# The first loads in smaller pieces: x's first columns ahead of wq, and wq's last chunks behind a DMA transpose

## The chip, the cores and the metric

The kernel runs on one core of one Trainium2 chip. The metric is the time of one execution on the device in microseconds (us); lower is better. The core has a matrix engine (TensorE, PE in the profile, with PEld for its weight loads), VectorE (DVE), ScalarE (ACT), GpSimd (POOL), and SyncE (SP), which here only issues DMAs. PE works on operands in on-chip memory and writes to eight banks of accumulation memory ("ps"), each of 128 x 512 fp32; DVE and ACT read the banks out. DMAs are issued by SP and ACT, each into a queue of its own, and both queues are served by the same 16 DMA engines.

## The reference

x is 2048 x 512. Two branches work on the same x and are mixed by a gate per row:

```python
g = _sigmoid((x * gate_w).sum(-1, keepdims=True))
a = _A_ref(x, A_wq, A_wk, A_wv, A_wo, A_beta)
b = _B_ref(x, B_W_gate, B_W_up, B_W_down)
return g * a + (1 - g) * b
```

`_A_ref` is attention with 32 heads of 16 columns, in four segments of 512 rows. In each segment there is a causal softmax over the segment itself, and a linear "memory" of all segments before: q and k pass through phi(t) = t + 1 where t > 0, else exp(t); M and z sum phi(k)^T v and phi(k); the memory's answer is phi(q) M / (phi(q) z). The two answers are mixed by a gate per head (from beta), and multiplied by wo. `_B_ref` is a feed-forward layer: relu(x W_gate) * (x W_up), times W_down, with 1792 inner columns. All weights and x are bf16.

## The kernel before

The work is a list of tasks: each task has an engine, a duration as its author reckons with it, the tasks it depends on, and a function that emits its instructions. The order in which the tasks are emitted is written out (`ORDER`, lines 30 to 93), and so is the choice of buffers (`UNITS`, lines 95 to 103). Each engine runs its instructions in that order, and semaphores make it wait for what it needs. So nothing is reordered at run time: an instruction that waits holds up all that stand behind it on its engine.

For q, k and the feed-forward layer x is needed transposed, as `xT`, with the 512 columns of x as four chunks of 128 partitions. q is projected in four column blocks c of 128 (8 heads each). Each block adds up four matmuls of 128 x 512, one for each chunk ci: weights `wq_sb[:, ci, block]`, moving operand `xT[:, ci, :]`. A projection can be emitted in full form (line 469) or as four matmuls of 32 columns (line 473), which run side by side; the second form is taken where the work before it ran in that mode. Score matmuls (lines 626 and 639), the sums over values (line 699) and the memory's matmuls (lines 755, 795, 819) work on parts of the matrix engine. Scores are kept in banks 0 to 3, where ACT takes the exponential of 2048 columns at once (line 648); the other work goes through banks 4 to 7 from then on.

The start of the first segment is made by hand, and it is there that the change lies:

- Warm-up (`heat`, lines 910 to 916): PE multiplies constants, six matmuls of 512 columns and one of 128, while the first loads are on their way.
- x's first 256 columns come as plain loads into `xn`, rows as partitions: "n0" (row tiles 0 and 1) in SP's queue, "n1" (row tiles 2 and 3) in ACT's (lines 300 and 301). PE transposes them by matmuls with an identity (`flip`, lines 504 to 508); DVE copies the tiles of n0 out into `xT[0]`, and ACT those of n1 (line 521).
- x's last 256 columns come through a DMA transpose straight into `xT[0]` (line 304), in SP's queue.
- wq's chunk 0 is loaded in SP's queue ahead of that transpose and chunk 1 in ACT's (lines 302 and 303); chunks 2 and 3 follow as one load in ACT's queue (line 306). wk in two halves, wv and all else follow in SP's queue.
- PE projects q with chunk 0 for all four blocks, then with chunk 1, then, for each block, with chunks 2 and 3 (lines 549 to 554). DVE copies each block out (line 559). k follows: DVE copies it out (line 575) and makes three masked forms of it (line 578), which the first score matmuls need.

```python
    got_n[0] = [load_x0(eng, 2 * t, 2 * t + 2, halves[0], "n%d" % t)
                for t, eng in enumerate((nc.sync, nc.scalar))]
    got_q = [load(eng, wq_sb[:, ci, :], A_wq[ci * P:(ci + 1) * P, :], "q%d" % ci)
             for ci, eng in enumerate((nc.sync, nc.scalar))]
    nc.sync.dma_start_transpose(out=xT[0][:, NC // 2:NC, :], in_=x[0:L, halves[1]])
    got_x0b = arrival("x0")
    got_q.append(load_rows(nc.scalar, wq_sb, A_wq, 1, "q"))
```

`LANDS` (line 258) are the arrival times of the loads that the written order was made with; they set nothing at run time.

Of the kernel before, what the change touches and what calls it, by code (L numbers as in the profile page):

```python
# [12 lines left out]
P = 128  # L13
S = 2048
D = 512
# [4 lines left out]
L = S // NSEG  # L20
F = 1792
NC = D // P
# [70 lines left out]
"""  # L93

UNITS = (
    "456701237654310000231213121203110023000000210000000310110000001000100002301130210110222232"
    "04301331053227100601183039303d120a312b223c001112003230031020230102221001012122101114563021"
    "000003200000002201100000310001000002011302221202231210a10231007323431253218203b32060029123"
    "d313c1102110032320020410232301120101322323031456710230000023000000032011000000200000000030"
    "1101300021211a31221238320311373225001630041129012b213d320c00121201222211023230202136272001"  # L100
    "1256210300000320000000330110000011000000075011312202201031020a2224303821033105322630071139"
    "002d713c124b11000210011"
)


class Slot:


    def __init__(self, cands):
        self.cands, self.units, self.left = tuple(cands), (), 0  # L110

    @property
# [66 lines left out]
def kernel(  # L179
# [15 lines left out]
    nc = tc.nc  # L195
# [58 lines left out]
    def work():  # L254
        return plan.one("ps", range(7, -1, -1))


    LANDS = dict(n0=3470, n1=3600, q0=4650, q1=4650, x0=6300, qb=6000, ka=7900, kb=9300,
                 v=11500, g0=13000, u0=14000, gw=14800, be=15100, g1=16300, u1=17500, n2=18500,
                 x1=21500, g2=22800, u2=23900, g3=25000, u3=26100, d0=28900, d1=31600, o=34400)  # L260

# [718 lines left out]
```

## Time and profile before

| | us |
|---|---|
| median of 3 runs | 263.92 (263.47 to 264.21) |
| the profiled execution | 264.48 |
| its span, first to last instruction | 262.7 |
| PE busy, 3828 matmuls | 257.8 (98%) |
| DVE busy | 204.9 (78%) |
| ACT busy | 183.7 (70%) |
| POOL busy | 64.2 (24%) |

The profile is of one execution. The page gives each engine's busy time; the list of waits says which engine stood, before which instruction, until what; the timeline lists instructions in order of time, those of one line and form merged, with start, duration and, in brackets, the idle time before them and what ended it. In it a matmul's form is rows * columns of the weights, then out <- in; "x12" means twelve instructions, and the duration runs from the first one's start to the last one's end. Matmuls overlap: each of 128 x 512 takes 0.38 us by itself, and a next one starts before it ends. A windows line gives, for a stretch, its length, then each engine's busy time and number of instructions in the order PE, PEld, DVE, ACT, POOL, then PE's granted clock, the DMA share and GB/s. The DMA view gives the rate in 40 equal slices of the window asked for.

### The profile page before, as it was taken

How to read it: one execution, taken by the hardware profiler on the slowest of the kernel's cores; microseconds unless marked ns; L12 is line 12 of the kernel's file. 1: busy time of each engine (PE TensorE's matmuls, PEld its weight loads, DVE VectorE, ACT ScalarE, POOL GpSimd, SP SyncE). 2: the span in 40 equal slices, each digit the busy share in tenths (PEclk: the TensorE clock that was granted, in tenths of full speed). 3: DMA queues.
4: the chain of work that ended last, by engine and by line, in shares of the span. 5: the costliest groups of instructions: out<-in, count | busy, mean ns of one | idle time of the engine just before them, and what ended most of it. 6: DMA issues, size and time to landing. Idle time of an engine off the chain costs nothing.

```text
span 262.7 us, 8841 instructions
## 1 busy us (share of the span) xinstructions
PE 257.8 (98%) x3828; PEld 117.4 (45%) x3828; DVE 204.9 (78%) x472; ACT 183.7 (70%) x168; POOL 64.2 (24%) x168
## 2 busy tenths in 40 slices
PE   8899999999999999999999999999999999999995
PEld 3344434454444454444444445444444444444454
DVE  2798999999995756959989789676998858688722
ACT  3199889999788678888486776878568759873000
POOL 8022732212321423232031223133121243121000
PEclk9999999999999999999999999999999999999999
DMA  6999984110711201200220111320110200311011
GB/s 146 337 304 323 273 192 53 22 24 10 116 25 52 92 22 39 76 2 2 80 41 4 56 20 36 110 85 2 24 57 3 56 2 22 102 30 73 2 42 42
DMA packets 31566, 19.72 MB, mean 75 GB/s; under 512 B 16040, under 2 KB 29992, under 8 KB 31528
## 3 DMA queue, kind: packets, MB, share of 16 engines
q1 hardware_dynamic: 30840, 18.64, 26.2%
q8 instruction: 30, 0.49, 0.9%
q10 hardware_dynamic: 688, 0.52, 0.9%
q14 instruction: 8, 0.07, 0.1%
HBM read 13.21 MB, written 2.55 MB: 60 GB/s over the span
## 4 chain that ended last, share of the span: by engine, by line
PE 94%; DMA 2%; DVE 2%; SPq 0%; issue 0%
PE ps L469 56%; PE ps L473 20%; PE ps L626 8%; PE ps L699 7%; DMA xT<-in_A_x_dram 2%; PE ps L639 1%; DVE QT L559 1%; PE ps L819 1%; PE ps L795 0%; PE ps L755 0%; SPq L266 0%; DVE KT L578 0%; DVE ktr L575 0%; DVE osr L895 0%
## 5 line engine op out<-in xcount | busy, mean ns | idle before, releaser
L648 ACT ACTIVATE E<-ps 128x2048 bf16<-128x2048 f32 x64 | 120.2, 1877 | 27.3 <-PE ps L626 18.8
L677 POOL TENSOR_SCALAR_AFFINE_SELECT E<-E 128x256 bf16<-128x256 bf16 x128 | 54.8, 452 | 169.8 <-ACT E L648 169.8
L869 DVE TENSOR_TENSOR hT<-ps,rgr 128x512 bf16<-128x512 f32 x56 | 38.0, 684 | 17.0 <-PE ps L469 12.6
L469 PE MATMUL ps<-xT,wu_sb 128*128 128x512 bf16 x168 | 45.9, 380 | 0.0
L469 PE MATMUL ps<-xT,wg_sb 128*128 128x512 bf16 x154 | 42.0, 380 | 0.0
L863 ACT ACTIVATE rgr<-ps 128x512 bf16<-128x512 f32 x56 | 32.5, 599 | 13.4 <-PE ps L473 6.9
L469 PE MATMUL ps<-wd_sb,hT 128*128 128x512 bf16 (+1 forms) x174 | 40.3, 354 | 0.0
L730 DVE STREAM_TRANSPOSE T<-ps 128x512 f32<-128x512 f32 x32 | 22.2, 707 | 7.8 <-PE ps L699 7.7
L626 PE MATMUL ps<-QT,KT 32*128 32x320 bf16 (+3 forms) x512 | 25.4, 273 | 0.1
L469 PEld LDWEIGHTS <-wu_sb 128*128 128x128 bf16 x168 | 15.1, 98 | 18.7 <-issue 2.7
L469 PEld LDWEIGHTS <-hT 128*128 128x128 bf16 x174 | 15.2, 98 | 17.1 <-issue 2.1
L469 PEld LDWEIGHTS <-wg_sb 128*128 128x128 bf16 x154 | 14.4, 98 | 17.7 <-issue 1.3
L895 DVE TENSOR_SCALAR osr<-ps,ngcol 128x512 bf16<-128x512 f32 (+2 forms) x18 | 12.2, 685 | 11.2 <-PE ps L473 5.7
L699 PE MATMUL ps<-E,Vp 128*17 128x320 bf16 (+3 forms) x512 | 19.3, 274 | 0.0
L626 PEld LDWEIGHTS <-KT 32*128 32x128 bf16 x512 | 7.6, 92 | 25.5 <-issue 24.2
L473 PE MATMUL ps<-xT,wg_sb 128*32 128x512 bf16 x280 | 18.6, 379 | 0.0
L648 ACT ACTIVATE Em<-ps 128x2048 bf16<-128x2048 f32 x8 | 15.0, 1876 | 5.0 <-PE ps L639 5.0
L473 PE MATMUL ps<-wd_sb,hT 128*32 128x512 bf16 (+1 forms) x312 | 17.8, 360 | 0.0
L469 PE MATMUL ps<-xT,wq_sb 128*128 128x512 bf16 x60 | 16.4, 382 | 1.0 <-DMA xT<-in_A_x_dram 1.0
L469 PE MATMUL ps<-wv_sb,xT 128*128 128x512 bf16 x62 | 16.9, 380 | 0.0
L559 DVE CAST QT<-ps 128x512 bf16<-128x512 f32 x16 | 10.7, 687 | 6.4 <-PE ps L469 6.2
L473 PE MATMUL ps<-xT,wu_sb 128*32 128x512 bf16 x224 | 15.1, 379 | 0.0
(102 smaller groups left out, 301.3 us busy)
## 6 DMA issues: line engine op xcount, KB each, us to landing
out_dram<-osr SPq DMA_DIRECT2D x15, 128.0 KB
wd_sb<-in_B_W_down_dram SPq DMA_DIRECT2D x2, 896.0 KB
xn<-in_A_x_dram SPq DMA_DIRECT2D x3, 512.0 KB
cdr<-coefs SPq DMA_DIRECT2D x6, 256.0 KB
xn<-coefs SPq DMA_DIRECT2D x6, 256.0 KB
wg_sb<-in_B_W_gate_dram SPq DMA_DIRECT2D x2, 512.0 KB
wu_sb<-in_B_W_up_dram SPq DMA_DIRECT2D x2, 512.0 KB
wg_sb<-in_B_W_gate_dram SPq DMA_DIRECT2D x2, 384.0 KB
```

The lines of the kernel that those rows point to most:

```text
L469: nc.tensor.matmul(out, lhsT=lhsT, rhs=rhs, start=start, stop=stop)
L473: nc.tensor.matmul(out[r], lhsT=lhsT[:, r], rhs=rhs, start=start, stop=stop, tile_position=(0, 32 * j))
L559: prj["q", seg, c] = plan.add("DVE", 600, key - RQK, lambda: nc.vector.tensor_copy(QT[i][:], bank(sl)), [a], DVL, frees=[sl])
L626: nc.tensor.matmul(ps[:, j * L + o:j * L + o + L - q], lhsT=KT[i][rows, kb, 3 * r:3 * r + 2].rearrange("p h q -> p (h q)"), rhs=QT[i][rows ...
L639: nc.tensor.matmul(ps[:, o:o + HP], lhsT=KT[i][rows, kb, 2:4].rearrange("p h q -> p (h q)"), rhs=QT[i][rows, kb * P:kb * P + HP], start=Tr ...
L648: last_exp[0] = [plan.add("ACT", 66 + 4 * L / 1.2, key, lambda: nc.scalar.activation(dst, ps[:, 0:4 * L], ACT.Exp, scale=SCALE), [a] + war ...
L677: nc.gpsimd.affine_select(out=m[:, :, o:o + HP], in_=m[:, :, o:o + HP], compare_op=ALU.is_ge, fill=0.0, base=HP, pattern=[[0, 4], [1, HP]] ...
L699: nc.tensor.matmul(bank(sl)[32 * m:32 * m + HW, q:q + w], lhsT=(Vp[i] if n < 4 else Vm)[:, kb, r, 4 * c + j, 0:HW], rhs=rhs, start=(n == 0 ...
L730: done.append(plan.add("DVE", 633, key - RL, lambda r=r, sl=sl: nc.vector.transpose(T[ts.i][:, r], bank(sl)), [a] + done, 75 if r else 0, ...
L863: r = plan.add("ACT", 478, key - RL, lambda sl=gsl, rs=rs: nc.scalar.activation(rgr[rs.i][:], bank(sl), ACT.Relu), [g], ACL, frees=[gsl])
L869: nc.vector.tensor_tensor(hT[hs1.i][:], bank(sl), rgr[rs.i][:], ALU.mult)),
L895: nc.vector.tensor_scalar(osr[os.i][:, n0 - c0:n1 - c0], bank(sl)[:, 0:n1 - n0], ngcol[:, tt:tt + 1], None, ALU.mult)),
```

## The change

x's first 256 columns come in four pieces instead of two, 128 columns by two row tiles each: n0 and n2 in SP's queue, n1 and n3 in ACT's, all ahead of wq. The PE transposes of a chunk wait for that chunk's own pieces. The warm-up has one matmul of 512 columns less, and its last one has 256 columns instead of 128. wq's chunks 2 and 3 are two loads in SP's queue, behind the DMA transpose, instead of one in ACT's. The first q projection adds chunk 2 for all blocks and then chunk 3, as separate tasks, each waiting for its own load. `LANDS`, `ORDER` and `UNITS` are written anew, so all engines have another order from the first projections to the end. In the emitted program, nine projection matmuls change from the four-part form to the full one; k's first two matmuls stand ahead of the last of q's, and two of v's matmuls ahead of the first score matmuls.

```diff
-    LANDS = dict(n0=3470, n1=3600, q0=4650, q1=4650, x0=6300, qb=6000, ka=7900, kb=9300,
-                 v=11500, g0=13000, u0=14000, gw=14800, be=15100, g1=16300, u1=17500, n2=18500,
-                 x1=21500, g2=22800, u2=23900, g3=25000, u3=26100, d0=28900, d1=31600, o=34400)
+    LANDS = dict(n0=3150, n1=3200, n2=3500, n3=3550, q0=4300, q1=4400, x0=6000, q2=6100,
+                 q3=6500, ka=7700, kb=8700, v=10900, g0=12500, u0=13800, gw=14800, be=15100,
+                 g1=16300, u1=17500, n4=18700, x1=21500, g2=22800, u2=23900, g3=25000, u3=26100,
+                 d0=28900, d1=31600, o=34400)
...
-    halves = slice(0, D // 2), slice(D // 2, D)
-    got_n[0] = [load_x0(eng, 2 * t, 2 * t + 2, halves[0], "n%d" % t)
-                for t, eng in enumerate((nc.sync, nc.scalar))]
-    got_q = [load(eng, wq_sb[:, ci, :], A_wq[ci * P:(ci + 1) * P, :], "q%d" % ci)
-             for ci, eng in enumerate((nc.sync, nc.scalar))]
-    nc.sync.dma_start_transpose(out=xT[0][:, NC // 2:NC, :], in_=x[0:L, halves[1]])
+    queues = nc.sync, nc.scalar
+    got_n[0] = [load_x0(eng, 2 * t, 2 * t + 2, slice(ci * P, ci * P + P), "n%d" % (2 * ci + t))
+                for ci in range(2) for t, eng in enumerate(queues)]
+
+    def load_wq(eng, ci):
+        return load(eng, wq_sb[:, ci, :], A_wq[ci * P:(ci + 1) * P, :], "q%d" % ci)
+
+    got_q = [load_wq(eng, ci) for ci, eng in enumerate(queues)]
+    nc.sync.dma_start_transpose(out=xT[0][:, NC // 2:NC, :], in_=x[0:L, D // 2:D])
     got_x0b = arrival("x0")
-    got_q.append(load_rows(nc.scalar, wq_sb, A_wq, 1, "q"))
+    got_q += [load_wq(nc.sync, ci) for ci in range(2, NC)]
...
-                a = plan.add("PE", 214, K(-9 + ci) + t, flip, [got_n[0][t]], PEL, need=[sl], size=4)
+                a = plan.add("PE", 214, K(-9 + ci) + t, flip, [got_n[0][2 * ci + t]], PEL, need=[sl], size=4)
...
-            a = matmuls(K(-4, c), [got_q[2]] + got_x[0][1], sl, proj_mm(wq_sb, c, 0)[2:], prev=a,
-                        start=False)
+            for ci in range(2, NC):
+                a = matmuls(K(-6 + ci, c), [got_q[ci]] + got_x[0][1], sl,
+                            [proj_mm(wq_sb, c, 0)[ci]], prev=a, start=False, stop=ci == NC - 1)
...
-        for k in range(7):
-            w = L if k < 6 else P
+        for k in range(6):
+            w = L if k < 5 else 2 * P
```

More of the change, by code (lines that the diff above doesn't have):

```diff
@@ L30 @@
 ORDER = """
[62 rows of a table removed]
[63 rows of a table added]
 """
 UNITS = (
[L96 to L102, printed above, removed]
+    "456701237654320001332101212203121310200000030000000120110000001000000002301121312000022302"
+    "34301201151207202621281029303d123a211b223c100102102020133100103232022101033100100145671203"
+    "000003200000002201100000210001000031011302211200231100732032238203431363129213c1005120a301"
+    "b022d0211110032320151600230322022301323222001345630210000013000000033011000003200030000230"
+    "112222112021033037223c203111092206003821142015100b001d012a10021201303121312220302243013031"
+    "205631020000002000000022011000003300000007101130332230112232372114300c32210026113532082019"
+    "312d126b304a11000210011"
 )
@@ L314 @@
     load_gu(1)
-    got_n[0].append(load_x0(nc.sync, 0, NC, halves[1], "n2"))
+    got_n[0].append(load_x0(nc.sync, 0, NC, slice(D // 2, D), "n4"))
     load_xT(1)
@@ L911, in heat @@
         one = nc.const_aps.tensor(1.0, (P, 1), BF16)
-        for k in range(7):
-            w = L if k < 6 else P
+        for k in range(6):
+            w = L if k < 5 else 2 * P
             nc.tensor.matmul(bank(warm[k])[:, 0:w], lhsT=one.to_broadcast([P, P]),
                              rhs=one.to_broadcast([P, w]), start=True, stop=True)
-    plan.add("PE", 3470, -1e9, heat, lat=0, need=warm, frees=warm, size=14)
+    plan.add("PE", 3150, -1e9, heat, lat=0, need=warm, frees=warm, size=14)
     got_x[0] = x0_tasks()
```

125 rows, old and new, of the table ORDER are left out of this document.

## The prediction

> **What bounds the kernel now.** I first read the page's busy times and slices, then the waits of PE, then the timeline of the first 13 us, then the DMA slices.
>
> ```profile
> span 262.7 us, 8841 instructions
> PE 257.8 (98%) x3828; PEld 117.4 (45%) x3828; DVE 204.9 (78%) x472; ACT 183.7 (70%) x168; POOL 64.2 (24%) x168
> ...
> 13.00:250.00 237.00, 237.00 (x3568) 106.17 (x3569) 195.60 (x449) 180.83 (x164) 58.76 (x144) 1.00 0.25 68
> ```
>
> ```profile
> PE ps L469 <- DMA xT<-in_A_x_dram: 1.0, 1, 1.0
> PE ps L914 <- PEq L964: 0.8, 1, 0.8
> ```
>
> PE is the bound: from 13 to 250 us it is busy for 237.00 of 237.00 us, and the list of its waits holds only the 0.8 us before its first instruction and one wait of 1.0 us for the transposed x. Only a different sum of PE work, a new wait, or the first 13 us can move the end.
>
> ```profile
> 0.84 2.83 PE L914 MATMUL ps<-const-bfloat16-1.0 128*128 128x512 bf16 x7 [0.84 <-PEq L964]
> 3.65 1.06 PE L506 MATMUL ps<-ident,xn 128*128 128x128 bf16 x8
> 4.75 2.01 PE L469 MATMUL ps<-xT,wq_sb 128*128 128x512 bf16 x8
> 7.73 1.89 PE L469 MATMUL ps<-xT,wq_sb 128*128 128x512 bf16 x8 [0.97 <-DMA xT<-in_A_x_dram]
> 9.45 2.75 PE L469 MATMUL ps<-xT,wk_sb 128*128 128x512 bf16 x12
> 12.34 0.40 PE L626 MATMUL ps<-QT,KT 32*128 32x448 bf16 x8
> ...
> 6.82 0.10 PEld L469 LDWEIGHTS <-wq_sb 128*128 128x128 bf16 x1 [0.55 <-DMA wq_sb<-in_A_wq_dram]
> 12.34 0.12 PEld L626 LDWEIGHTS <-KT 32*128 32x128 bf16 x8 [0.63 <-DVE KT L578]
> ```
>
> The eight first-half q matmuls are through by 6.6; then PE stands until 7.73, with wq's last chunks there (weights load at 6.82) and the transpose not. The chain of waits has that transpose as "1.82 5.87": issued 1.82, landed 7.69. The first score batch waits for DVE, which is busy without a break from the first q copy on:
>
> ```profile
> 8.36 2.48 DVE L559 CAST QT<-ps 128x512 bf16<-128x512 f32 x4 [3.40 <-PE ps L469]
> 10.76 0.68 DVE L575 CAST ktr<-ps 128x512 bf16<-128x512 f32 x1
> 11.48 0.35 DVE L578 TENSOR_SCALAR KT<-ktr,mcol_o 128x512 bf16<-128x512 bf16 x1
> ```
>
> DMA rate in quarter microseconds from 0 to 10, from 15 to 25, and in eighths from 64 to 69:
>
> ```profile
> GB/s 0 0 0 0 0 0 0 41 82 111 272 352 359 373 357 221 173 205 274 243 151 69 57 50 212 197 224 336 308 188 336 357 344 348 336 369 344 332 360 356
> ...
> GB/s 348 340 356 352 340 356 312 336 287 261 289 291 286 290 293 290 268 127 68 108 144 276 344 301 320 350 366 378 356 375 363 378 313 332 338 323 329 327 344 338
> ...
> GB/s 0 0 0 0 0 0 0 0 0 0 0 88 225 227 223 227 188 164 260 285 291 293 289 293 285 295 285 218 45 14 0 0 0 20 152 213 215 219 188 42
> ```
>
> Between 4.0 and 7.1 the transpose (SyncE's queue) and wq's chunks 2 and 3 (ScalarE's) share the engines, and from 5.0 to 6.0 the rate falls to 50 to 151 GB/s. The third line is a transpose alone: issued at 64.09, first bytes at 65.4, then 164 to 295 GB/s.
>
> **The change part by part.** Times are from the span's start; T1 is when PE starts the first matmul on transposed x, 7.73 now.
>
> *Steady work.* In the built programs, nine projection matmuls pass from four-column form (L473) to full form (L469): 672 to 681 full, 952 to 916 quarters. Twelve full take 2.75 us, so 11 steps and one duration of 0.38: 0.215 each; the sixteen quarters at 44.31 take 1.04, so three steps and 0.38: 0.22 for four. The 64 score batches and 8 diagonal ones, each a change of mode, are the same. Sum: nothing, within 0.05 us.
>
> *Warm-up and x in four pieces.* Warm-up loses some 0.3 us (one matmul step of 0.43, with the last one 128 columns wider, 0.11). PE now waits for landings instead. x's first half still is 262 KB, in 256-byte runs: such run at 290 GB/s where plain loads do 350, 0.15 us more, and I take 0.2 for everything behind. ScalarE's queue issues three DMAs as before. The eight first-half matmuls then end between 6.3 (pieces 0.3 earlier) and 6.9 (last piece 0.3 later); I take 6.6 as now. This gains nothing by itself: PE would only stand longer in front of the transpose.
>
> *Transpose.* Its issue moves back by one DMA (0.45 and a gap of 0.06) to 2.33. Issue to first byte is 1.3 alone (64.09 to 65.4), which gives 3.6; now its first packets run at 4.05, behind wq's chunk 0 in that queue. The bytes ahead are the same, so 4.05 + 0.2 = 4.25; the other end keeps today's 2.23 from the issue, 4.55. Alone, 262 KB need 1.2 us (sum of the third line from 65.4 to 66.6) where they now take 3.05 (4.05 to 7.1). Last packet to landing is 0.55 now (7.15 to 7.69). So it lands at 6.0 to 6.3.
>
> *wq's chunk 2 behind it.* 131 KB at 350 GB/s is 0.37. What follows a transpose is slowed: after the half one now, the 188 among 336s (7.25) is 0.12 us; after the whole one at 19.25 the slices 127, 68, 108, 144, 276 against 345 lose 250 KB, 0.73 us. I take 0.15, from the transpose of the same size. Chunk 2 lands at 5.45 + 0.15 + 0.37 + 0.55 = 6.52, or 6.82 from the late end: T1 is 6.7, with ends 6.6 and 7.4.
>
> *Behind that.* Chunk 3 is 0.37 later, 7.1; it is needed four matmuls after T1, at 7.56. wk's halves (0.75 each) land near 7.8 and 8.6; needed seven and ten matmuls after T1, 8.2 and 8.9. SyncE's queue holds three more DMAs ahead of wk, 1.5 us: its issue goes from 3.18 to 4.75, still 1.8 us ahead of its bytes. wv and the rest move no bytes later, so what now lands ahead of use stays so.
>
> *DVE.* q's first copy starts after five matmuls instead of two (chunk 2 of all four columns, then chunk 3): T1 + 4 x 0.216 + 0.41 = T1 + 1.28, instead of 0.63. From first copy to first score batch is 12.34 - 8.36 = 3.98, with the same eight DVE instructions, so the batch starts at T1 + 5.26. PE reaches it after 22 matmuls (two of v are now ahead of it), T1 + 4.85, and stands 0.41 instead of 0.21. The gain is 12.34 + 0.43 (those two) - 5.26 - T1 = 7.51 - T1 = 0.8 us.
>
> *ACT.* Its second exp now has two more exps of k ahead: from the batch 0.46 + 1.77 + 1.1 + 0.5, and 1.77 itself, 5.6; the third batch comes at two periods of 3.03 (12.34, 15.37, 18.40), 6.06. Covered by 0.4 us; without that cover PE would wait for what is over.
>
> **Sum.** 0.8 us off the profiled execution's 264.48 (span 262.7 and 1.8 around it) is 263.7; that execution is 0.56 above the runs' median, so the median goes from 263.92 to 263.1.
>
> **Rivals.**
> *B, the transpose shares little of its time.* If it gains only what its neighbour's bytes cost (262 KB at 350 GB/s, 0.75 us), it lands at 7.69 + 0.3 - 0.75 = 7.25 and chunk 2 at 7.6: T1 7.6, 264.0; the full slowing of 0.73 behind it gives T1 7.4, 263.8. Against: 3.05 us for 262 KB is far more than fair sharing with another 262 KB. [...]
>
> *C, slower: the transpose is slow by itself.* If the 3.05 us are its own, and so the dip, it lands at 7.95 and chunk 2, now behind it, at 8.3: 264.7. It decides from a transpose of 2.9 us on. For: in the dip both queues starve. Against: alone at 65.4 it ran 225 GB/s from its second slice.
>
> *D, slower: PE stays at half rate.* Warm-up matmuls step by 0.43 us, the last flips by 0.107 at 128 columns, and the 0.216 steps begin at 5.1, 4.2 us after PE's start. With gaps in the warm-up the eight matmuls could all take 0.43: 1.7 us more, T1 8.3, 264.7. Against: PE's stand of 1.0 us before 7.73 left 0.216 steps behind it. [...]
>
> *E, slower: the new order waits somewhere.* All engines' orders are new after the first matmuls. One instruction put behind one exp too many costs 1.77 us: 263.1 + 1.8 = 264.9. For: the score batches leave ACT a few tenths. Against: today's order has no such wait in 237 us, with the same tasks and durations.
>
> **How the numbers follow.** My forecast 0.56 (own range 262.8 to 263.5), of which 0.36 beyond 0.3% (0.79 us, about what a measurement of this kernel can tell from no change; T1 under 6.72) and 0.20 within; B 0.18, within; C 0.09, D 0.05, E 0.12, slower but for 0.02 within. So faster 0.36, same 0.40, slower 0.24. The range runs from T1 6.4 (262.8) to E (264.9); it leaves out half of E and the tails.
>
> **What would show it.** Right: no dip between the transpose's first packets and its landing, T1 at 6.6 to 7.0, the first score batch 5.2 to 5.3 us after T1 with KT as its releaser, no further PE waits. Wrong: the transpose landing after 7.3 (B, C), 0.43 us steps after 5.3 (D), any PE wait on ACT or DVE after 13 us (E), or a last matmul that isn't earlier by what T1 shows.

## The result, and the profile after

The changed kernel takes 266.8 us at the median of eight runs (264.97 to 269.76), the kernel before beside it 264.12 (263.47 to 264.24). The ratio is 1.0084, with an interval of 1.0067 to 1.0101: slower by 2.2 us, where 263.1 was forecast, and past the end of the range. Two of the eight, at 269.6 and 269.8, are not in the ratio, because they stand apart from the other six at a lower granted clock (0.993 and 0.994 against 0.999 to 1.0); the profile below is of one of these two, so what it shows at 43 us is not the size of the loss in the others, and a second profile, of an execution of 267.4, is shown further down.

The start, in the timeline of TensorE (start, duration, what, idle time before it and what ended it):

```profile
4.88 3.42 PE L474 MATMUL ps<-xT,wq_sb 128*128 128x512 bf16 x15 [0.60 <-DMA wq_sb<-in_A_wq_dram]
8.66 0.59 PE L474 MATMUL ps<-xT,wk_sb 128*128 128x512 bf16 x2 [0.35 <-DVE QT L565]
9.09 0.38 PE L474 MATMUL ps<-xT,wq_sb 128*128 128x512 bf16 x1
9.50 2.33 PE L474 MATMUL ps<-xT,wk_sb 128*128 128x512 bf16 x10
11.67 0.59 PE L474 MATMUL ps<-wv_sb,xT 128*128 128x512 bf16 x2
12.20 0.40 PE L632 MATMUL ps<-QT,KT 32*128 32x448 bf16 x8
...
6.62 1.19 PEld L474 LDWEIGHTS <-wq_sb 128*128 128x128 bf16 x7 [0.33 <-DMA wq_sb<-in_A_wq_dram]
```

The last line, of the weight loads, shows where the ninth of q's matmuls begins, the first on transposed x. Here the start went nearly as forecast: the transpose landed at 5.87 instead of 7.69, that matmul began at 6.62 (forecast 6.7) when wq's chunk 2 was there, and the first score batch came at 12.20 with two of v's matmuls (0.43) ahead of it, which is a gain of 0.57 over before's 12.34, where 0.8 was forecast. The loss of this execution is elsewhere. The list of waits, and the windows of the page's core (length, busy times of PE, PEld, DVE, ACT, POOL, then PE's granted clock, DMA share, GB/s):

```profile
DVE junk L428 <- DMA xn<-in_A_x_dram: 4.7, 1, 4.7
PE ps L474 <- DVE T L736: 3.7, 1, 3.7
```

```profile
13.00:43.00 30.00, 30.00 (x341) 12.77 (x343) 27.75 (x85) 28.20 (x31) 11.26 (x34) 1.00 0.91 242
43.00:52.00 9.00, 5.31 (x73) 2.21 (x66) 4.64 (x12) 3.58 (x3) 2.01 (x4) 0.81 0.78 52
52.00:250.00 198.00, 197.45 (x3037) 90.09 (x3039) 159.22 (x346) 148.62 (x131) 44.67 (x106) 1.00 0.15 42
```

Nine microseconds, 43 to 52, hold nearly all of it. The timeline there, first VectorE's and then TensorE's lines:

```profile
47.26 0.84 DVE L428 SCALAR_TENSOR_TENSOR junk<-xn,gwb 128x512 bf16<-128x512 bf16 x1 [4.68 <-DMA xn<-in_A_x_dram]
48.03 1.30 DVE L736 STREAM_TRANSPOSE T<-ps 128x512 f32<-128x512 f32 x2
```

```profile
44.69 0.40 PE L632 MATMUL ps<-QT,KT 32*128 32x320 bf16 x8
48.79 1.01 PE L474 MATMUL ps<-xT,wg_sb 128*128 128x512 bf16 x2 [3.69 <-DVE T L736]
49.59 1.06 PE L474 MATMUL ps<-xT,wu_sb 128*128 128x512 bf16 x2
```

VectorE stands 4.68 us for x's rows of segment 1 (`xn`, loaded by `load_xn(1)`, used for the row gates). It works in order, so the copy of `T`, for which TensorE needs the bank, stands behind it; TensorE is idle for 3.69 us and then runs at half rate, in steps of 0.43 us until 51.3 and of 0.216 from 51.6 on (granted clock 0.81 in this window). SyncE's own timeline tells why the load is late, of the kernel after and then of the kernel before:

```profile
34.30 3.83 SPq L597 DMA_TRANSPOSE pK<-pkT  x3
38.18 1.93 SPq L275 DMA_TRANSPOSE xT<-in_A_x_dram  x1
40.22 0.52 SPq L278 DMA_DIRECT2D xn<-in_A_x_dram  x1
```

```profile
32.57 1.26 SPq L591 DMA_TRANSPOSE pK<-pkT  x1
33.94 0.51 SPq L276 DMA_DIRECT2D xn<-in_A_x_dram  x1
34.51 3.19 SPq L273 DMA_TRANSPOSE xT<-in_A_x_dram  x1
```

In the new order the xn load stands behind three pK transposes and the transpose of segment 2's x. It is issued at 40.22 instead of 33.94 and lands at 47.23 instead of 37.91. The queue also starts this stretch 1.7 us later. Its first pK transpose waits for the last part of the load of wd: the trace counts each load in 16 parts, and the last of wd's comes at 34.22 instead of 32.49.

In this execution the load was slow besides: 7.0 us from issue to landing, where the second profile further down has 4.5 (40.26 to 44.78) in the same place. The DMA rate, in quarter microseconds from 38 to 48, is next to nothing from 44.25 to 47.0:

```profile
GB/s 68 220 208 29 0 0 79 183 265 282 283 276 270 291 284 167 270 221 238 324 318 329 259 181 156 15 0 0 0 4 12 8 16 25 20 18 232 273 10 0
```

Why is not shown. By an estimate from these two landings, some 2.4 us of the wait of 4.68 come from it, and the rest from the place in the queue.

### The profile page after: what moved, and what is told of

The parts are those of the page before. It is cut to its first block, busy times and chain, and to the rows that moved or that the text cites. A ratio compares the mean times of both kernels' runs of the same rounds, so it can differ in the third digit from the quotient of the medians.

```text
span 268.0 us, 8781 instructions
## 1 busy us (share of the span) xinstructions
PE 259.1 (97%) x3800; PEld 118.5 (44%) x3800; DVE 204.4 (76%) x472; ACT 183.4 (68%) x168; POOL 63.4 (24%) x168
## 4 chain that ended last, share of the span: by engine, by line
PE 91%; DMA 4%; ACT 2%; DVE 1%; issue 1%; SPq 0%; DVEq 0%; ACTq 0%
PE ps L474 57%; PE ps L478 18%; PE ps L632 7%; PE ps L705 6%; DMA xn<-in_A_x_dram 3%; ACT E L654 1%; DMA wq_sb<-in_A_wq_dram 1%; PE ps L645 1%; PE ps L825 1%; DVE T L736 1%; PE ps L761 0%; PE ps L801 0%; SPq L268 0%; ACT rgr L869 0%; DVE QT L565 0%
## 5 line engine op out<-in xcount | busy, mean ns | idle before, releaser
L474 PE MATMUL ps<-xT,wg_sb 128*128 128x512 bf16 x160 | 44.4, 383 | 3.7 <-DVE T L736 3.7
L474 PE MATMUL ps<-xT,wu_sb 128*128 128x512 bf16 x172 | 47.0, 383 | 0.0
L474 PE MATMUL ps<-wd_sb,hT 128*128 128x512 bf16 (+1 forms) x173 | 41.4, 354 | 0.0
L474 PEld LDWEIGHTS <-wg_sb 128*128 128x128 bf16 x160 | 15.1, 99 | 22.6 <-issue 6.1
L474 PEld LDWEIGHTS <-wu_sb 128*128 128x128 bf16 x172 | 15.9, 98 | 19.7 <-issue 2.7
L478 PE MATMUL ps<-xT,wg_sb 128*32 128x512 bf16 x256 | 17.8, 379 | 0.0
L474 PE MATMUL ps<-xT,wk_sb 128*128 128x512 bf16 x58 | 16.8, 388 | 0.5 <-DVE QT L565 0.4
L474 PE MATMUL ps<-xT,wq_sb 128*128 128x512 bf16 x54 | 15.1, 380 | 0.6 <-DMA wq_sb<-in_A_wq_dram 0.6
L428 DVE SCALAR_TENSOR_TENSOR junk<-xn,gwb 128x512 bf16<-128x512 bf16 x16 | 11.2, 702 | 4.9 <-DMA xn<-in_A_x_dram 4.7
```

Source lines behind the costliest of these rows:

```text
L428: zs.append(plan.add("DVE", 690, key, lambda t=t: nc.vector.scalar_tensor_tensor(junk[:], xn[:, t, :], 1.0, gwb[:], ALU.mult, ALU.mult, ac ...
L474: nc.tensor.matmul(out, lhsT=lhsT, rhs=rhs, start=start, stop=stop)
L478: nc.tensor.matmul(out[r], lhsT=lhsT[:, r], rhs=rhs, start=start, stop=stop, tile_position=(0, 32 * j))
```

## The experiments

Three causes were proposed after this profile: xn's place in SyncE's queue (theory A below), the new loads (rival L), and several faults of the new order (rival O). The first four kernels undo or do one part each; "pK", "xn" and "xT2" stand for the tasks of `ORDER` that issue these DMAs.

**e1: the changed kernel with xn forward.**

```diff
 # what SyncE issues from 33 us on
-pK  pK  pK  xT2  xn  pK
+pK  xn  pK  pK  xT2  pK
```

> The changed kernel with one task moved: the load of segment 1's x rows (xn) is issued by SyncE right behind the first of the pK transposes, as in the kernel before, instead of behind three of them and behind the transpose of segment 2's x. Theory A (the start gained some 0.6 us as the first score batch shows, and the loss is this load's place in the queue, with VectorE and then TensorE standing for it): no wait of VectorE for xn over 0.3 us, no wait of TensorE for T at 43 to 49 us, time 263.2 to 263.8, under the kernel before. Rival L (the loads in their new sizes leave all later transfers late, wherever they stand): xn still lands 6 to 7 us after its issue, the wait at VectorE shrinks but others come, 265 to 266. Rival O (the new order has several small faults, of which this is the one that shows in the profiled run): 264.5 to 266.

Measured: 265.84 us against 264.01, ratio 1.0062 (1.0043 to 1.0081). In its profile (264.82 us) xn lands at 38.35 and neither VectorE nor TensorE waits for it; beside the changed kernel's, VectorE's 103 instructions up to the wait end at the same time within 0.15 us, and those behind it 4.8 to 5.0 us earlier. So the wait is settled, and its price in that execution was 5.0 us, the slow load included. But the six other executions of the changed kernel have a median of 266.4, only 0.5 us above e1, and 1.8 us are left over the kernel before: theory A is not the whole.

**e2: the kernel before with xn back.**

```diff
-pK  xn  xT2  pK  pK  pK
+pK  pK  pK  xT2  xn  pK
```

> The kernel before with the same task moved the other way: segment 1's xn load stands behind three pK transposes and behind the transpose of segment 2's x. VectorE uses it first at 38.4 us here. Theory A: it is issued near 39 instead of 33.9 and lands at 43 to 46, VectorE stands 4 to 7 us, TensorE less, by what it still has to do without VectorE: 266 to 271. Rival O or L: the load's place is no matter by itself, within 0.5 us of the kernel before, 264.1.

Measured: 269.08 us against 264.01, ratio 1.0192 (1.0172 to 1.0212). xn lands at 41.86, where VectorE wants it at 38:

```profile
DVE junk L421 <- DMA xn<-in_A_x_dram: 3.9, 1, 3.9
PE ps L467 <- DVE hT L867: 3.2, 1, 3.2
```

Theory A's number: this place alone costs 5 us where VectorE uses xn early.

**e3: the new loads, the old order. e4: the old loads, the new order.**

```diff
 # e3: the changed kernel, with before's ORDER and UNITS, tasks renumbered
 # e4: the kernel before, with the changed kernel's ORDER and UNITS, tasks renumbered
```

> The loads, warm-up and split q matmuls of the changed kernel alone: all tasks stand in the order, and use the banks and buffers, of the kernel before, with chunk 3's matmul of a block right behind chunk 2's. Theory A: the gain of the start without the loss: 263.0 to 263.6, no wait of VectorE for xn. Rival L (the loads do it): 265 or more, with late landings at 32 us and after. If the old order can't use the earlier start at all: 264.1.

> The order and the choice of banks of the changed kernel alone, on the loads, the warm-up and the paired q matmuls of the kernel before. Theory A: the loss without the gain: 265.5 to 268, VectorE waits for xn at 42 us and after. Rival L: 264.1 to 264.5, no such wait.

Measured: e3 264.60 (263.99 to 266.11), ratio 1.0021 (1.0006 to 1.0037); e4 264.76 (264.21 to 265.27), ratio 1.0022 (1.0010 to 1.0033). Both halves lose some 0.6 to 0.75 us and neither gains, against every theory. In e4 xn stands at the late place as well, and lands at 42.72, where VectorE's work reaches it at 42.5: a wait of 0.2 us. So with the old loads the late place is just harmless in this order; in the changed kernel's first profile the load was issued 1.9 us later and took longer.

e4's profile shows what the order costs by itself. It is one stand, in the middle of a sum over values, that nothing in the profile explains:

```profile
107.92 0.28 PE L698 MATMUL ps<-Em,Vm 128*17 128x64 bf16 x10
109.16 0.23 PE L698 MATMUL ps<-Em,Vm 128*17 128x64 bf16 x6 [0.97 <-issue]
```

"issue" means that no wait is recorded. The changed kernel's own profile has it at the same matmuls, after the 43 us trouble:

```profile
113.13 0.28 PE L705 MATMUL ps<-Em,Vm 128*17 128x64 bf16 x11
113.83 0.22 PE L705 MATMUL ps<-Em,Vm 128*17 128x64 bf16 x5 [0.43 <-issue]
```

The page's DMA queues suggest what it is:

```profile
q8 instruction: 29, 0.48, 0.8%
```

29 packets of 16 KB: taken to be TensorE's program, brought while it runs. Their starts in the trace lie 256 of TensorE's instructions apart on average (the kernel before has 30; the first starts at its 195th instruction, the last at its 7612th). At 105.2 us TensorE runs 150 instructions in 0.84 us; in e4 the piece that belongs there starts at 106.85, and the stand ends at 109.16. The kernel before has such a place too, but its piece started 2.3 us ahead of it (103.98, place from 106.23). The stands are given below as what the step from one matmul to the next takes over its usual length: 1.16 us here, 0.62 in the changed kernel.

e3's profile (266.11 us) is late from the start: the first score batch comes at 13.98 instead of 12.34, all after it takes as long as before. Its first matmuls stepped by 0.43 us until 9.75.

The next four kernels test both readings, a piece of the program that comes late and a start at half rate.

**e5: e3 with TensorE kept busy at the start.**

```diff
                     for k in range(2):
                         (transpose of a tile)
+                    for k in range(2 if t and not ci else 0):
+                        nc.tensor.matmul(bank(sl)[:, 2 * P:4 * P], lhsT=junk[:, 0:P], ...)
...
-                        one multiplication of junk behind the last transpose
+                        three of them
```

> The new loads with the order of the kernel before (e3), and TensorE kept busy at the start: two more multiplications of zeros by 256 columns between the transposes of x's first and second chunk, and three instead of one behind the second. Theory H (e3's profiled run was late because its matmuls ran at half rate, steps of 0.43 us until 9.75, after TensorE stood 0.42 and 0.49 us for its first loads; the full rate begins 4 to 6 us after TensorE's start where it has no such gaps): the steps of 0.216 begin by 7.7 us in the profile, no run over 265.2, median 263.4 to 264.1, under e3's 264.6. Rival J (e3's spread comes from the loads' landing times alone): as e3, median 264.4 to 264.8 with runs over 265.4, and half-rate steps past 8 us may stay.

Measured: 265.52 (264.56 to 266.09), ratio 1.0043 (1.0026 to 1.0060). The steps of 0.216 do begin at 5.03 and the first score batch comes at 11.64, earlier than in any other kernel with these loads; so the start was as theory H expects in this execution, and its forecast of the time was wrong. What was gained came back as waits for loads that were no earlier:

```profile
DVE junk L426 <- DMA xn<-in_A_x_dram: 1.6, 1, 1.6
PE ps L472 <- DVE hT L878: 0.8, 1, 0.8
PE ps L472 <- DMA wg_sb<-in_B_W_gate_dram: 0.4, 1, 0.4
```

**e6: e4 with 72 more instructions ahead of 105 us. e7: the kernel before with 60 less.**

```diff
-                t.col = bool(t.flex) and mode == "col"
+                t.col = bool(t.flex) and (mode == "col" or t.n in SIX)     # e6: six tasks in four-part form
+                t.col = bool(t.flex) and mode == "col" and t.n != 577     # e7: this and the four behind it in full form
```

> The old loads with the new order (e4), and six projection tasks (two matmuls each) just ahead of the dense place at 105.5 us turned from the full form into the four-part form: 72 more instructions in TensorE's stream. Theory F (the 0.97 us that TensorE stood at 108.2 us in e4, between two matmuls of one sum over values and waiting for nothing the profile shows, is a 16 KB piece of its instructions, 256 of them, that was asked for too late because 200 instructions run in 1.4 us there): with the boundary of the pieces at another place the stand is gone, 263.9 to 264.2, like the kernel before. Rival G (the stand is of the new order itself, or the 0.75 us are spread over it): 264.6 to 264.9, and the stand remains.

> The kernel before with five projection tasks (two matmuls each) ahead of the same dense place turned from the four-part form into the full form: 60 instructions less in TensorE's stream, nothing else. Theory F: the boundary of the instruction pieces comes to lie where the dense place begins, as in the changed kernel, TensorE stands 0.4 to 1.1 us near 108 us, 264.4 to 265.2. Rival G: no stand, 264.0 within 0.2.

Measured: e6 264.94 (263.78 to 265.78), ratio 1.0029 (1.0012 to 1.0045); e7 264.48 (263.99 to 265.09), ratio 1.0015 (1.0004 to 1.0025). In e6 the stand at 108 us is gone, and there is one at the second dense place, which lies behind the shift too:

```profile
205.02 0.31 PE L625 MATMUL ps<-QT,KT 32*128 32x320 bf16 x2
206.26 0.39 PE L625 MATMUL ps<-QT,KT 32*128 32x320 bf16 x6 [0.94 <-issue]
```

In e7 a stand came up where before had none, at 108.79, but of 0.31 us only, a little under the expected 0.4; its median is 0.36 over before's, within the expected range. Rival G expected the stand to remain in e6 and none in e7; that is refuted. The time did not yet follow, since the fault had moved.

**e8: all three mended at once** (e1, with e5's and e6's edits).

> The changed kernel with all three mended: segment 1's xn load behind the first pK transpose (e1), TensorE kept busy at the start (as e5), and 72 more instructions ahead of the dense place (as e6). If xn's place, the half-rate start and the instruction piece are the whole loss: 263.2 to 263.9, under the kernel before. If something else of the new order or of the new loads costs time as well: 264.3 or more.

Measured: 265.61 (265.40 to 266.39), a miss: it has e6's stand at 204.94, of 1.67 us there. Its start brought nothing either: the first score batch came at 12.78.

**e9: e4 with both dense places mended.**

```diff
+                six tasks ahead of 105 us in four-part form (as e6)
+                six tasks between 112 and 175 us in full form
```

> The old loads with the new order (e4), with the 72 more instructions ahead of the dense place at 105 us (as e6) and 72 less between 112 and 175 us, so that the second dense place, at 202 us, stands to the boundaries of the instruction pieces as in e4 (in e6 TensorE stood 1.2 us there instead of at 108). Theory F: neither stand, and the new order by itself costs nothing: 263.7 to 264.3, as the kernel before. Rival G: the order costs its 0.7 us some other way: 264.6 to 265.

Measured: 264.23 (264.03 to 264.66) against 264.16, ratio 1.0008 (0.9999 to 1.0017). No stand at either place. e4 without them was at 1.0022: with the old loads the new order costs nothing else that these runs can tell (the interval ends at 0.4 us).

**e10: e1 with e9's edit**, that is the changed kernel with xn and the instruction pieces mended and its loads as they are.

> The changed kernel with segment 1's xn load behind the first pK transpose (e1) and the same two moves of the instruction boundaries (e9), its start as it is. Theory F with the start as in e3: 0.6 to 1.2 us under e1's 265.84, so 264.6 to 265.2, and what is left over the kernel before is the new loads' start. Rival G: as e1, 265.6 to 266.0.

Measured: 264.86 (264.29 to 266.60), ratio 1.0035 (1.0016 to 1.0054). 0.7 us are left, about as much as in e3 (0.6), so they are the loads'. From e1 it is 1.0 us by the medians and 0.7 by the ratios; two profiles of e1 show a stand of 0.55 and 0.74 us. If there is a rest, it is not explained.

**e1 and the changed kernel once more**, for second profiles.

> e1 once more, for a profile of an execution nearer to its median than the first one, which was 1.0 us under it. If the start makes e1's spread: the first score batch comes up to 1.8 us later than 12.30 with steps of 0.43 us past 7 us, the rest as before, one stand of 0.5 to 1.2 us near 108 us. If not: waits after 13 us that the first profile doesn't show.

> The changed kernel once more, for a profile of an execution other than the 269.8 one. If the xn load decides each time: VectorE waits for xn, 1 to 5 us, the longer the later wd's last part landed ahead of SyncE's first pK transpose, and the stand at 108 us is there too.

e1: 265.01 us, the first score batch at 12.35 and the stand of 0.74. The expected half-rate start was not in this execution. It was in the changed kernel's second one (267.38):

```profile
4.00 0.42 PE L520 MATMUL ps<-junk 128*128 128x256 bf16 x1
5.19 5.60 PE L474 MATMUL ps<-xT,wq_sb 128*128 128x512 bf16 x15 [0.78 <-DMA wq_sb<-in_A_wq_dram]
11.14 0.59 PE L474 MATMUL ps<-xT,wk_sb 128*128 128x512 bf16 x2 [0.35 <-DVE QT L565]
```

Fifteen matmuls in 5.60 us, where the first profile has 3.42. The first score batch came at 14.47. xn landed at 44.78 and VectorE used it at 44.80, with no wait: this execution was 2.3 us late at the start and did not have to wait for xn. The expectation that xn decides each time was wrong; of these two executions the one paid for xn (4.68 us of wait) and the other for its start. The stand was there in both, 0.77 us in this one.

Then the loads were taken apart, in the order of the kernel before.

**e11: wq's chunks 2 and 3 behind the transpose, alone. e12: x in four pieces, alone.**

```diff
 # e11: e3 with
+    x's first 256 columns as two loads, seven matmuls of warm-up
 # e12: the kernel before with
-    n0: 256 columns in SP's queue, n1: 256 columns in ACT's
+    128 columns in SP's, 128 in ACT's, the next 128 in SP's, in ACT's
```

> Of the new loads only wq's chunks 2 and 3 as two loads behind the transpose in SyncE's queue, with the split q matmuls; x in two pieces, the warm-up and the order of the kernel before. Theory P (the four pieces of x, with runs of 256 bytes, leave one part of each load late): here the parts land within 0.3 us of each other, the transpose lands at 6.0 to 6.3 and q's chunk 2 starts by 6.9 instead of 7.2 to 7.9; the first score batch comes by 11.6, and 263.4 to 264.0 follow, unless VectorE then waits for xn. Theory Q (the transpose that runs alone, with loads waiting behind it, leaves the part late): parts 0.5 to 1.2 us late from wq's chunk 2 on, 264.2 to 264.9.

> Of the new loads only x's first 256 columns in four pieces ahead of wq; all else is the kernel before (TensorE waits for all pieces of two row tiles). Theory P: one part of the loads from wq on lands 0.5 us and more behind the others, and the time is 264.3 to 265. Theory Q: the parts land together as before, 264.0 to 264.3, with everything at most 0.2 us later.

Measured: e11 263.94 (263.52 to 264.81), ratio 1.0004 (0.9989 to 1.0018); e12 263.60 (263.17 to 266.19), ratio 0.9993 (0.9974 to 1.0012). Neither is slower. In e11 the transpose landed at 5.63, but the parts of the loads behind it came apart (wv's last part 2.14 us behind its median part), as theory Q has it; the time is under Q's range and within P's. So late parts do not cost time in every order. In e12 one part of wq's chunks 0 and 1 was 1.4 us late in the profiled execution (266.19, half-rate steps until 9.93), and later loads were together again; the time is under both theories' ranges.

**e13: e3 with the long warm-up. e14: e3 with wq's last chunks in ScalarE's queue. e12 once more.**

```diff
 # e13
-        for k in range(6):
-            w = L if k < 5 else 2 * P
+        for k in range(7):
+            w = L if k < 6 else P
 # e14
-    got_q += [load_wq(nc.sync, ci) for ci in range(2, NC)]
+    one load of both chunks in ScalarE's queue, as before
```

> e3 (the new loads in the order of the kernel before) with the warm-up of the kernel before: six matmuls of 512 columns and one of 128. Theory W (the short warm-up does the harm, because the first matmuls then stand and run at half rate longer): 263.4 to 263.9, as e11 and e12 added up. Theory X (the two halves of the loads harm each other): as e3, 264.4 to 264.8.

> e3 with wq's chunks 2 and 3 as one load in ScalarE's queue, as in the kernel before; x in four pieces and the short warm-up stay. Theory W: 264.3 to 264.8, with late executions over 265.5. Theory X: as e12, 263.4 to 263.8.

> e12 once more: x in four pieces alone. If it is a gain: 263.4 to 263.8 again, a ratio under 1 with its interval, but for single executions near 266 whose first matmuls run at half rate until 10 us. If e12's median was luck: 264.0.

Measured: e13 264.53, ratio 1.0024 (1.0008 to 1.0040); e14 263.86 (263.16 to 265.68), ratio 1.0007 (0.9988 to 1.0027); e12 again 263.68 (263.19 to 264.24), ratio 0.9987 (0.9977 to 0.9996). The long warm-up changes nothing (e3 had 264.60), and wq's old place mends the median: theory X, the two halves together. How they harm each other is not shown beyond the profiles. e14 still has three executions of twelve at 265.5 to 265.7, such as theory W expected; none of them was profiled. e13's profile has TensorE waiting 1.02 us for wv, the load behind wk:

```profile
11.81 0.40 PE L630 MATMUL ps<-QT,KT 32*128 32x448 bf16 x8
13.23 1.02 PE L472 MATMUL ps<-wv_sb,xT 128*128 128x512 bf16 x4 [1.02 <-DMA wv_sb<-in_A_wv_dram]
```

**e15: e10 with wq's chunks 2 and 3 back in ScalarE's queue.**

> e10 (the changed kernel with segment 1's xn load and the instruction boundaries mended) with wq's chunks 2 and 3 as one load in ScalarE's queue, as in the kernel before. If their place behind the transpose is all that is left of the loss: 263.5 to 263.9, as e12 and e14, the parts of wv landing within 0.4 us of each other. If the new order needs them early, or something else is left: 264.4 to 264.9, as e10.

Measured: 264.17 us against 264.18, ratio 1.0001 (0.9988 to 1.0013). wv's parts are 0.13 us apart. The loss is gone, though the gain of e12 does not show in this order. Its first matmul on transposed x begins when e14's does (7.14 and 7.15), but its first score batch comes at 12.49 against 11.76. Of that, 0.43 are v's two matmuls; the other 0.3 go with k's first matmul, which stands until 9.16 for the bank that q's first copy frees.

One version comes out ahead of both kernels, if barely: e12, x in four pieces and nothing else. By its second runs it is 0.3 us faster than the kernel before; its first runs, with one execution at 266.19, have an interval that holds 1. In its profile of 263.47 us q's matmuls begin at 5.13, the transpose lands at 6.89 and the first score batch comes at 11.55.

## Why the prediction was wrong, point by point

Four steps of the prediction failed: the gain of 0.8 us, which does not come even where nothing else is lost (e15); the slowing behind the transpose, sized at 0.15 us; "what now lands ahead of use stays so", which was wrong for the loads behind wq and for xn; and the nine matmuls in another form, which were put at nothing. What the steps between the two kernels cost, from the medians and from the ratios, each beside the kernel before as measured with it:

| kernel | over before, us | ratio |
|---|---|---|
| e15: x in pieces, short warm-up, new order; xn and instruction pieces mended | 0.0 | 1.0001 (0.9988 to 1.0013) |
| e10: and wq's chunks 2 and 3 behind the transpose | +0.7 | 1.0035 (1.0016 to 1.0054) |
| e1: and the instruction pieces as the new order has them | +1.8 | 1.0062 (1.0043 to 1.0081) |
| the changed kernel: and xn behind the transposes | +2.7 (+2.2 by the ratio) | 1.0084 (1.0067 to 1.0101) |

The intervals of the first two rows are apart. Those of the other rows overlap with their neighbours; that these steps are real rests on the traces, on the stand at 108 us and the wait for xn, and on e9 and e2.

- **Steady work unchanged: right**, as far as matmul durations go. The step that failed stood beside it: the nine matmuls that pass from four-part to full form were costed at 0.215 us against 0.22, "nothing". They also take 54 instructions out of TensorE's stream, and with the new order the dense place comes some 60 instructions earlier in it, at another distance from the start of a packet of 16 KB. e7 made such a stand with an edit of this kind alone, e9 removed it with the contrary one. The price, by the ratios and by the medians beside before, is 0.4 to 0.7 us with the old loads (e4 to e9), 0.7 to 1.1 with the new ones (e1 to e10).
- **"T1 is 6.7": right in the profile (6.62), and wrong as a gain.** T1 was held against the one execution shown, 7.73. The six profiles with the old loads have 7.73, 7.26, 7.27, 7.87, 7.19 and 7.36: 7.45 on average. Six with the new loads in the new order (the changed kernel and e1 twice each, e8, e10) have 6.62, 8.58, 6.58, 6.98, 7.20 and 8.04: 7.33. The profiled execution of before was 0.56 us over the median, and from its first score batch to its last matmul it took 247.22 us, as e3's and e12's did (247.22, 247.20): its excess lay in the very stretch that the change shortens. So a part of the 0.8 us had already been left out of the median from which they were taken.
- **The transpose alone takes 1.2 us and lands at 6.0 to 6.3: nearly**, 5.87 in the first profile, 5.75 to 6.48 in those six. Rivals B and C, by which it would land after 7, are refuted.
- **wq's chunk 2 lands 0.52 behind the transpose (0.15 for the slowing, 0.37 for its bytes): mis-sized.** In the same six profiles its last part came 0.71 to 1.51 us behind the transpose, 1.07 on average. The prediction had two rows for the slowing, 0.12 and 0.73, and went by the first; the second would have given 1.10. In e10's profile it put T1 at 8.04: chunk 2 was complete at 7.99, its last part 1.17 us behind its median part, and the first score batch came at 13.40 against 12.49 in e15.
- **"wv and the rest move no bytes later, so what now lands ahead of use stays so": wrong.** With x in pieces, wq's place behind the transpose cost 0.7 us (e15 to e10); with x in two pieces it cost nothing (e11). It also prepared xn's stand. It was argued from bytes, but TensorE waited for the last of a load's 16 parts: in the first profile 14 of the parts of wk's second half were there by 8.47, the last at 9.45, and the matmul that uses it began at 9.50. In the ten profiles without wq behind the transpose, wv's last part came 0.05 to 0.42 us after its median part, in the ten with it 0.46 to 2.79 us. The loads stayed late: the last load of the first stretch (wo) was complete at 33.3 to 34.2 without it, at 34.6 to 37.0 with it. From there SyncE's queue goes on with pK, xT2 and xn, and so the xn load of the changed kernel was issued at 40.22 and 40.26 instead of e4's 38.35. The new place of xn had no slack (0.2 us of wait in e4), so in the first profile the lateness became a stand; in the second TensorE was as late as the load. SyncE's queue was followed for the first 5 us and not at 33.
- **An earlier start wants its loads earlier, too.** Where the start did get ahead with wq behind the transpose (e5 by 0.7 us, e13), TensorE and VectorE waited for loads. Both had late parts of wv (1.33 and 2.79 us). Where wq had its old place, e12's second profile and e14's got ahead as well (first score batch at 11.55 and 11.76) and waited for no load afterwards; so the late parts, and not the earlier use alone, go with these waits.
- **VectorE's chain from T1 to the first score batch, 5.26: right for VectorE, wrong for TensorE.** The first copy began at 7.91, T1 + 1.29 (forecast 1.28), and the masked forms of k that the batch needs were there at 11.84. But TensorE reached the batch only at 12.20, T1 + 5.58, where 4.85 was forecast and VectorE was to be the later one. k's first matmul had stood until 8.66 for q's first copy, which frees its bank, and the third of k until 9.50 for wk's second half (last part 9.45). These cost 0.5 and 0.2 us; the prediction has neither wait.
- **ScalarE's second exp is covered by 0.4 us: right**, as no wait of TensorE for ScalarE is in the changed kernel's list.
- **Rival D, half rate, chance 0.05: far too small a chance.** Its matmuls step by 0.43 until 9.4 to 9.9 us in three of thirteen profiles with x in four pieces (the changed kernel's second, e3, e12), in none of seven without. It priced T1 at 8.3; the changed kernel's execution that shows it has 8.58. The prediction saw that TensorE would stand between warm-up and q's matmuls, and set rival D aside because a stand of 1.0 us in before had full rate behind it; but that one came after the full rate had been reached (steps of 0.216 from 5.1). In the three late executions TensorE stood 0.78 to 0.96 us in all while still at half rate.
- **Rival E, the new order waits somewhere, chance 0.12: the right side, for other reasons.** It looked for an instruction behind one exp too many. What waited was VectorE for a DMA, held up in SyncE's queue by other DMAs, and TensorE, it seems, for its own program. "Today's order has no such wait" spoke of an order with other places of its DMAs.

## What to carry to other kernels

When loads move, follow each queue to its end and not only past the change: ask of every later load in it by how much it lands ahead of its first use, and price a new order by those slacks. Take the gain of a shorter start from several executions, since one profile's late start is partly the luck that the median has already left out. And when a stand has no wait recorded, hold it against the packets of the instruction queue: here 60 instructions less, far upstream, brought one of 0.31 us (e7), and 72 more took one of 1.16 us away (e6).

## What the runs showed of the hardware

- **What is taken to be TensorE's program came in packets of 16 KB, and a dense place seems to have outrun them.** In before's trace there are 30 such packets, 256 of TensorE's instructions apart on average. With the boundaries counted as in the kernel before, places where 150 instructions take 0.7 to 0.9 us that begin 31 to 43 or 111 to 114 instructions behind a boundary had no stand (before, e12, e6, e9, e10, e15, and the second place of the changed kernel); those that begin 186 to 235 behind it stood 0.31 (235, e7), 0.55 to 1.16 (215: the changed kernel, e1 and e4), 1.24 and 1.67 us (186 and 191, e6 and e8). When a piece is asked for is not in the trace, and no kernel tried other shifts.
- **Loads queued behind a DMA transpose that had the engines to itself landed with their 16 parts apart**: wv's last part came 0.46 to 2.79 us behind its median part, 5 us behind the transpose. Where the transpose shared its time with a load of the other queue, it came within 0.42 us. In some profiles one or two parts are late, in others half of them; why was not shown.
- **The half rate of TensorE's first matmuls (steps of 0.43 us, then 0.216) ended at different times.** Matmuls begin at 0.84 us in all. In 17 profiles the steps became short between 3.6 and 6.6 us; in the three late ones between 9.4 and 10.3, with nothing between the two groups. A stand did not decide it by its length alone: 0.78 to 0.96 us at half rate in the three, but 0.40 and 0.57 in e12's second profile and e14, which rose at 5.1 and 5.7, and in e10 1.19 us with full rate right behind it. With the stands of 3.69 us up to 48.79 (the changed kernel's first profile) and of 3.17 up to 43.49 (e2) came a granted clock of 0.50 for 3.41 us each, from 48.01 to 51.42 and from 44.08 to 47.49. What ends the half rate was not shown.
